# First group of a block-sparse attention and SwiGLU kernel: order of values and transposes, pace of the FFN pieces

## The chip, the core and the metric

The kernel runs on one core of one Trainium2 chip. The metric is device time in microseconds of one execution; the time before is the median of three runs. The engines are TensorE (PE in the profile, its weight loads PEld), VectorE (DVE), ScalarE (ACT), GpSimd (POOL) and SyncE (SP), which issues DMAs, as POOL does too. They run side by side, each in its own order, and wait for each other by semaphores.

## The reference

```python
# q, k, v: (4, 8, 768, 64) float32; block = 32, n_blocks = 24
scores = scale * np.matmul(q, k.transpose(0, 1, 3, 2))
# mask: neighbouring blocks, first and last block row and column,
#       and three sampled key blocks for each query block
scores = np.where(mask, scores, -1000000000.0)
scores = scores - np.max(scores, axis=-1, keepdims=True)
attn = np.exp(scores)
attn = attn / (np.sum(attn, axis=-1, keepdims=True) + 1e-09)
attn_out = np.matmul(attn, v)
x = attn_out.transpose(0, 2, 1, 3).reshape(B * S, H * D)        # 3072 x 512
rms = np.sqrt(np.mean(x * x, axis=-1, keepdims=True) + 1e-06)
xn = x / rms * rms_g
g = xn @ w_gate                                                 # 512 x 1536
out = (g * (1.0 / (1.0 + np.exp(-g))) * (xn @ w_val)) @ w_out   # 1536 x 512
```

## The kernel before

Queries, keys and weights are used in bf16. The work is cut into nine groups: the first batch into three groups of two 128-row chunks of queries, each of the other three batches into two groups of three chunks. The loop goes over the groups (`gi`), and in each over the eight heads (`h`). The order of all instructions is written out by hand: an engine runs what the program says next for it.

For one head, `scores` (L285) multiplies keys by queries in two parts (three in a large group) into one of two score tiles in PSUM. The mask needs no pass of its own: 24 extra rows, in partitions 64 to 87 of the transposed keys `KT` and queries `QT`, add a large negative number to what is masked. ACT takes the exponential of each part into `ex` (L297). `pv` (L301) multiplies `ex` by the values `Vp`, which have a column of ones for the sum, into the tile `op`, and DVE normalizes it into `stage` (L310, L311). In the code before, `pv` of a head comes one head later, behind that head's two parts of scores.

The tile `op` stands in a PSUM pool with a single buffer (`ps_o`, tag `ot`). Another pool (`ps_f`, tag `ff`) has three buffers and holds everything else that TensorE writes: gates, values, down-projections, fillers and some of the transposes.

After the last `pv` of a group, `squares` (L315) and `rms_power` (L323) make the root mean square, `rms_scale` (L334) writes `xs`, and the transposed `xg` comes by TensorE (`transpose_x`, L348) for the three groups of the first batch and for the last group, and by a DMA transpose from SP's queue for the five others. `enter` then puts the group's FFN pieces in a list, `fill`: for each of 12 blocks of 128 hidden columns a gate piece (L375) and a value piece (L386), then for each chunk four down pieces (L403). A head has four places (`position`) from which pieces are drawn:

```python
    def enter(e, positions):
        fill.extend(ffn_pieces(ps_f, e["grp"], e["xg"]))
        rate[0] = len(fill) / positions
```

So the FFN of one group lies between the attention of the next. What is left in the list when attention ends is drained, and the last group's FFN follows.

In the first group there are no pieces yet. Keys and queries of pair 0 (heads 0 and 1) come in float32 by SP's queue and are cast and transposed at once (`first_cast`, `first_turn`, `first_copy`). Pairs 1 to 3 and the values are loaded by POOL's queue in the order k, q, v of each pair, then the weights; from the ninth load on, POOL waits before a load for the landing of the one eight before it. `transpose_qk` (L246) turns a pair of loaded heads by TensorE, `copy` brings the result into `KT` or `QT` (L262). Of the queries, the first chunks are turned ahead of the group that needs them, the rest later (`hi` and `lo`). `cast_v` (L102) casts the values of a pair. `keep_busy` (L145) issues matmuls whose result nobody reads, "fillers" in what follows. `side_work`, `turn_first`, `casts` and `turns` hold what is done beside a head. The other batches are turned by DMA transposes from SP's queue (`turn`, `place`).

Of the kernel before, what the change touches and what calls it, by code (L numbers as in the profile page):

```python
# [18 lines left out]
def kernel(  # L19
# [17 lines left out]
    nc = tc.nc  # L37
    P = 128
    B, H, S, D = q.shape
# [9 lines left out]
    HC = NC // 2  # L49
# [73 lines left out]
    def first_cast(h, which):  # L123
        t16 = ld.tile([P, NC * D], BF16, name="t16", tag="t16", bufs=4)
        nc.scalar.copy(out=t16, in_=first[(h, which)])
        return t16

    def first_turn(t16, lo, hi, unread=None):
# [98 lines left out]
    nc.sync.dma_start(out=QT[0][D:KR, 2:H, 0:2 * P],  # L227
                      in_=qmask[:, 0:2 * P].unsqueeze(1).to_broadcast([NB, H - 2, 2 * P]))
    unread = ps_s.tile([P, 1024], FP32, name="unread0", tag="st")
    keep_busy(8, 256, unread)  # L230
    k16 = first_cast(0, 0)
    kt = first_turn(k16, 0, HC, unread)
    q16 = first_cast(0, 1)
    qt = first_turn(q16, 0, 1, unread)
    keep_busy(5, 256, unread)
    first_copy(0, 0, kt, 0, 0, HC, nc.scalar.copy)
    first_copy(0, 0, kt, 1, 0, HC, nc.vector.tensor_copy)
    first_copy(0, 1, qt, 0, 0, 1, nc.scalar.copy)
    first_copy(0, 1, qt, 1, 0, 1, nc.vector.tensor_copy)
    second16 = [first_cast(1, which) for which in range(2)]  # L240
    mask_keys(HC, NC)
    nc.sync.dma_start(out=KT[0][D:KR, 4:H, :],
                      in_=kind.unsqueeze(1).to_broadcast([NB, H - 4, S]))


    def transpose_qk(pr, which, lo, hi, spare, copy):  # L246

        b = 0  # L250
        src = (kbf if which == 0 else qbf)[(b, pr)]
        dst = (KT if which == 0 else QT)[b % 2]
        pool, tag = (ps_f, "ff") if spare else (ps_o, "ot")
        t = pool.tile([P, 2, HC, P], BF16, name="tqk", tag=tag)
        for e in range(2):
            for cc in range(lo, hi):
                nc.tensor.transpose(  # L257
                    out=t[:, e, cc, :], in_=src[:, e, 2 * cc * D:(2 * cc + 2) * D],
                    identity=ident)
        view = dst[0:D, 2 * pr:2 * pr + 2, :].rearrange("p e (c w s) -> p e c w s", w=2, s=P)  # L260
        for w in range(2):
            copy(out=view[:, :, lo:hi, w, :], in_=t[w * D:(w + 1) * D, :, lo:hi])  # L262
# [180 lines left out]
            if fill:  # L443
                fill.pop(0)()

    prev = None
    ending = None

    def after_pv(e, h):
        if h == H - 2:  # L450
            squares(e, 0, 0, (H - 1) * D)
        if h == H - 1:
            for it in range(e["grp"][2]):
                squares(e, it, (H - 1) * D, H * D)
            rms_power(e)

    def side_work(gi, h):

        if gi == 0:
            if h == 0:  # L460
                copy_rows(KT, kind, 2, 4, 0, S)
            if h % 2 == 0:
                cast_v(0, h // 2, nc.vector)
            if h == 1:
                load_gv(NF // 2, NF)
                nc.gpsimd.dma_start(out=wo, in_=moe_w_out.rearrange("(c p) f -> p c f", p=P))
            if h == 1:
                for third in range(1, FIRST):
                    mask_queries(third)
                nc.sync.dma_start(  # L470
                    out=QT[0][D:KR, 1:H, 2 * P:S],
                    in_=qmask[:, 2 * P:S].unsqueeze(1).to_broadcast([NB, H - 1, S - 2 * P]))
        if gi == 1:
            if h == 1:
                load_qk(1, 0)
                load_v(1, 0)
                load_v(1, 1)
                load_qk(1, 1)
            if h == 3:
                nc.gpsimd.dma_start(  # L480
                    out=gain, in_=moe_rms_g.unsqueeze(0).to_broadcast([P, DM]))
                load_qk(1, 2)
            if h == 5:
                load_qk(1, 3)
        if gi == 2 and h == 1:
            for T, m in ((KT, kind), (QT, qmask)):
                nc.gpsimd.dma_start(out=T[1][D:KR, :, :],
                                    in_=m.unsqueeze(1).to_broadcast([NB, H, S]))

    def turn_first(gi, h):  # L490


        if gi == 0 and h == 0:
            transpose_qk(1, 0, 0, HC, True, nc.vector.tensor_copy)
        if gi == 0 and 0 < h < H - 2:
            if h % 2:
                transpose_qk(h // 2 + 1, 1, 0, 1, True,
                             nc.scalar.copy if h < 4 else nc.vector.tensor_copy)
            else:
                transpose_qk(h // 2 + 1, 0, 0, HC, True, nc.vector.tensor_copy)  # L500
        if gi == 0 and h >= H - 2:
            e = h - (H - 2)
            t = first_turn((q16, second16[1])[e], 1, HC)
            for w in range(2):
                first_copy(e, 1, t, w, 1, HC, nc.vector.tensor_copy)
        if gi == 1 and h in (0, 2, 4):
            transpose_qk(h // 2 + 1, 1, 1, HC, h == 0, nc.vector.tensor_copy)

    def casts(gi, b, g, h):

# [16 lines left out]
    def turns(gi, b, g, h):  # L527


        ready = next(iter(turned), None)  # L530
        if gi == FIRST - 1:
            turn(1, h // 2, h % 2)
        if 0 < b < B - 1 and h >= 4:
            turn(b + 1, 2 * g + (h - 4) // 2, h % 2)
        if ready is not None:
            place(*ready)
# [3 lines left out]
    for gi, grp in enumerate(groups):  # L540
# [8 lines left out]
        for h in range(H):  # L549
            ex = ex_tile(n)  # L550
            thin = gi == 0 or (gi == 1 and h <= TX)
            if gi == 0 and h in (1, 2):
                keep_busy(2, 512)
            scores(grp, h, 0, ex)
            if h == 0 and prev is not None and prev[0]["grp"][2] == HC:
                squares(prev[0], 2, 0, (H - 1) * D)
            if gi == 0 and h == 0:
                scores(grp, h, 1, ex)
                second = [first_turn(t16, 0, 1 if which else HC)
                          for which, t16 in enumerate(second16)]  # L560
                copy_rows(KT, kind, 1, 2, 0, S)
                copy_rows(QT, qmask, 1, 2, 0, 2 * P)
# [34 lines left out]
            if gi == 0 and h == 0:  # L597
                turn_first(gi, h)
# [5 lines left out]
            if gi == 1:  # L604
# [13 lines left out]
            prev = (cur, h, ex)  # L618
    pe, ph, pex = prev
    squares(pe, 2, 0, (H - 1) * D)  # L620
    pv(pe["grp"], ph, pex, pe["stage"])
    after_pv(pe, ph)

    def drain(left):
        while len(fill) > left:
# [44 lines left out]
```

## Time and profile before

| what | value |
|---|---|
| median of three runs | 316.76 us (316.76 to 317.07) |
| profiled execution | 317.04 us |
| its span, first to last instruction | 315.3 us |
| mean granted TensorE clock | 0.997 |
| TensorE busy | 306.1 us (97%) |
| VectorE busy | 202.4 us (64%) |
| ScalarE busy | 207.7 us (66%) |
| fillers (L150) | 43 matmuls, 14.1 us |
| first gate piece starts at | 28.80 us |
| first down piece starts at | 47.9 us |

Times in the trace are microseconds from the start of the span. A row of the timeline gives start, duration, engine, source line, operation, the tile written and those read, the shape, the number of merged instructions, and in brackets how long the engine had been idle and what ended that. Busy times count the rows themselves; matmuls overlap in the array, so the spacing of the starts says more than the length of a row.

### The profile page before, as it was taken

How to read it: one execution, taken by the hardware profiler on the slowest of the kernel's cores; microseconds unless marked ns; L12 is line 12 of the kernel's file. 1: busy time of each engine (PE TensorE's matmuls, PEld its weight loads, DVE VectorE, ACT ScalarE, POOL GpSimd, SP SyncE). 2: the span in 40 equal slices, each digit the busy share in tenths (PEclk: the TensorE clock that was granted, in tenths of full speed). 3: DMA queues.
4: the chain of work that ended last, by engine and by line, in shares of the span. 5: the costliest groups of instructions: out<-in, count | busy, mean ns of one | idle time of the engine just before them, and what ended most of it. 6: DMA issues, size and time to landing. Idle time of an engine off the chain costs nothing.

```text
span 315.3 us, 7295 instructions
## 1 busy us (share of the span) xinstructions
PE 306.1 (97%) x2875; PEld 202.2 (64%) x2875; DVE 202.4 (64%) x560; ACT 207.7 (66%) x337; POOL 50.0 (16%) x75
## 2 busy tenths in 40 slices
PE   7998999999999999999999999999999999989995
PEld 5676886886787566655666566655666566645553
DVE  6778875776478647782767457682767446674850
ACT  6796775877788676657676676666766766723321
POOL 9626032100220122012110122010000100010000
PEclk9999999999999999999999999999999999999998
DMA  6999999995787589615784368615000220002002
GB/s 142 265 246 209 208 268 174 203 174 125 204 151 129 115 185 150 128 23 152 135 158 94 85 166 143 133 30 149 3 2 0 72 81 2 3 6 94 2 0 101
DMA packets 66754, 37.12 MB, mean 118 GB/s; under 512 B 48544, under 2 KB 62312, under 8 KB 66720
## 3 DMA queue, kind: packets, MB, share of 16 engines
q0 software_dynamic: 14976, 17.76, 30.4%
q1 hardware_dynamic: 51708, 18.89, 27.4%
q8 instruction: 22, 0.36, 0.5%
q14 instruction: 12, 0.10, 0.1%
q10 hardware_dynamic: 36, 0.01, 0.0%
HBM read 28.59 MB, written 6.29 MB: 111 GB/s over the span
## 4 chain that ended last, share of the span: by engine, by line
PE 92%; DVE 3%; DMA 2%; ACT 1%; issue 0%; POOL 0%; DVEq 0%; ACTq 0%
PE gp L375 20%; PE vp L386 19%; PE st L294 19%; PE yp L403 19%; PE op L306 11%; PE unread L150 2%; DVE junk L318 2%; DMA first<-in_k_dram 1%; DMA xg<-xs 1%; PE tx L357 1%; PE tqk L257 1%; DVE stage L311 1%; DVE u L390 0%; PE tfirst L131 0%; DVE hps L392 0%
## 5 line engine op out<-in xcount | busy, mean ns | idle before, releaser
L297 ACT ACTIVATE ex<-st 128x768 bf16<-128x768 f32 x192 | 154.2, 812 | 55.6 <-PE st L294 53.6
L294 PE MATMUL st<-QT,KT 88*128 88x384 bf16 (+1 forms) x432 | 94.5, 310 | 0.9 <-DVE QT L262 0.6
L375 PE MATMUL gp<-xg,wg 128*128 128x384 bf16 (+1 forms) x432 | 80.7, 307 | 0.7 <-DMA xg<-xs 0.7
L390 DVE SCALAR_TENSOR_TENSOR u<-th,gp 128x384 bf16<-128x384 bf16 (+1 forms) x108 | 54.8, 508 | 40.3 <-ACT th L379 38.7
L386 PE MATMUL vp<-xg,wv 128*128 128x384 bf16 (+1 forms) x432 | 80.2, 307 | 0.4 <-DVE u L390 0.4
L403 PE MATMUL yp<-wo,hps 128*128 128x512 bf16 (+1 forms) x300 | 74.0, 370 | 0.7 <-DVE hps L392 0.7
L379 ACT ACTIVATE th<-gp 128x384 bf16<-128x384 f32 (+1 forms) x108 | 48.9, 453 | 28.6 <-PE gp L375 28.4
L392 DVE TENSOR_TENSOR hps<-u,vp 128x384 bf16<-128x384 bf16 (+1 forms) x108 | 55.1, 510 | 12.5 <-PE st L294 0.5
L294 PEld LDWEIGHTS <-KT 88*128 88x128 bf16 x432 | 42.0, 99 | 26.1 <-DVE QT L262 0.8
L375 PEld LDWEIGHTS <-wg 128*128 128x128 bf16 x432 | 40.3, 97 | 21.3 <-issue 1.1
L386 PEld LDWEIGHTS <-wv 128*128 128x128 bf16 x432 | 40.5, 97 | 20.8 <-issue 0.8
L306 PEld LDWEIGHTS <-ex 128*128 128x128 bf16 x1152 | 46.1, 98 | 10.2 <-DVE stage L311 0.5
L306 PE MATMUL op<-Vp,ex 128*128 128x65 bf16 x1152 | 48.8, 194 | 0.1
L403 PEld LDWEIGHTS <-hps 128*128 128x128 bf16 x300 | 27.7, 97 | 23.6 <-DVE hps L392 1.2
L310 DVE RECIPROCAL rz<-op 128x3 f32<-128x3 f32 (+1 forms) x72 | 12.5, 174 | 28.8 <-PE op L306 28.4
L326 POOL TENSOR_TENSOR rstd<-ssq,mhalf 128x3 f32<-128x3 f32 (+1 forms) x9 | 7.3, 815 | 146.0 <-DVE ssq L318 146.0
L311 DVE TENSOR_TENSOR stage<-op,rz 128x192 bf16<-128x192 f32 (+1 forms) x72 | 24.1, 335 | 2.5
L409 ACT ACTIVATE yo<-yp 128x512 f32<-128x512 f32 (+1 forms) x25 | 14.4, 576 | 17.0 <-PE yp L403 17.0
L84 POOL DMA_DIRECT2D vraw<-in_v_dram x16 | 11.9, 747 | 70.1 <-DVE Vp L103 54.4
L150 PE MATMUL unread<-idle 128*128 128x512 bf16 (+1 forms) x43 | 14.1, 406 | 1.2 <-DVE idle L143 1.2
L318 DVE CUSTOM_DVE_ANT_0 junk<-stage 128x448 bf16<-128x448 bf16 x24 | 15.0, 623 | 0.6
L338 DVE SCALAR_TENSOR_TENSOR xs<-stage,rstd,gain 128x512 bf16<-128x512 bf16 x15 | 10.4, 747 | 4.4 <-POOL rstd L326 4.4
(59 smaller groups left out, 102.2 us busy)
## 6 DMA issues: line engine op xcount, KB each, us to landing
vraw<-in_v_dram POOLq DMA_DIRECT2D x16, 384.0 KB, 5.8
out_dram<-yo SPq DMA_DIRECT2D x23, 256.0 KB, 2.4
kbf<-in_k_dram POOLq DMA_DIRECT2D x15, 192.0 KB, 6.4
qbf<-in_q_dram POOLq DMA_DIRECT2D x15, 192.0 KB, 6.6
KT<-turned SPq DMA_DIRECT2D x24, 96.0 KB, 3.7
QT<-turned SPq DMA_DIRECT2D x24, 96.0 KB, 2.4
wo<-in_moe_w_out_dram POOLq DMA_DIRECT2D x1, 1536.0 KB, 25.0
wg<-in_moe_w_gate_dram POOLq DMA_DIRECT2D x2, 384.0 KB, 10.6
```

The lines of the kernel that those rows point to most:

```text
L150: nc.tensor.matmul(out=t[:, 0:cols], lhsT=idle[:, 0:P], rhs=idle[:, 0:cols], start=True, stop=True)
L294: nc.tensor.matmul(out=at[:, e, 0:tg], lhsT=KT[b % 2][0:KR, h, jt * P:(jt + 1) * P], rhs=QT[b % 2][0:KR, h, c0 * P:c0 * P + tg], start=Tru ...
L297: nc.scalar.activation(out=ex[:, nj * part:nj * (part + 1), :], in_=at[:, 0:nj, 0:tg], func=AF.Exp, scale=SCALE)
L306: nc.tensor.matmul(out=op[:, it, 0:VW], lhsT=ex[:, jt, it * P:(it + 1) * P], rhs=Vp[b % 2][:, h, jt, :], start=(jt == 0), stop=(jt == NC - 1))
L311: nc.vector.tensor_tensor(out=stage[:, 0:n, h * D:(h + 1) * D], in0=op[:, 0:n, 0:D], in1=rz[:, 0:n].unsqueeze(2).to_broadcast([P, n, D]), ...
L318: nc.vector.tensor_tensor_reduce(out=junk[:, 0:hi - lo], in0=part, in1=part, scale=1.0, scalar=(e["ssq"][:, it:it + 1] if lo else DM * 1e- ...
L375: nc.tensor.matmul(out=gp[:, 0:tg], lhsT=wg[:, c, f * P:(f + 1) * P], rhs=xg[:, c, 0:tg], start=(c == 0), stop=(c == KD - 1))
L379: nc.scalar.activation(out=th[:, 0:tg], in_=gp[:, 0:tg], func=AF.Tanh, scale=0.5)
L386: nc.tensor.matmul(out=vp[:, 0:tg], lhsT=wv[:, c, f * P:(f + 1) * P], rhs=xg[:, c, 0:tg], start=(c == 0), stop=(c == KD - 1))
L390: nc.vector.scalar_tensor_tensor(out=u[:, 0:tg], in0=th[:, 0:tg], scalar=1.0, in1=gp[:, 0:tg], op0=ALU.add, op1=ALU.mult)
L392: nc.vector.tensor_tensor(out=hps[:, f, 0:tg], in0=u[:, 0:tg], in1=vp[:, 0:tg], op=ALU.mult)
L403: nc.tensor.matmul(out=yp, lhsT=hps[:, f, tt * P:(tt + 1) * P], rhs=wo[:, f, lo:hi], start=(f == 0), stop=(f == NF - 1))
```

## The change

In the first group, `pv` comes two heads later instead of one, ahead of the second part of scores; the last head does two. The transposes of pairs 1 to 3 come at other heads and behind the second part of scores, except at head 1. The casts of the values come at heads 1, 3, 5 and 6 instead of 0, 2, 4 and 6. The query copies of pair 2 go from ACT to DVE, as does one cast of pair 0. From head 1 on, the heads of the group have fewer fillers (one each from head 2 on, two at head 1, where there were two, and four at heads 1 and 2); the start has twelve in front instead of eight, and two instead of five ahead of the first scores. The rest of the queries of pairs 1, 2 and 3 is turned at head 7 of group 0 and heads 0 and 2 of group 1, instead of heads 0, 2 and 4 of group 1, and the second of these now takes the single buffer. The first FFN is spread over 44 positions instead of 36, and each later one over 34 instead of 32. Pair 0 of the second batch is turned by TensorE at heads 5 and 6 of the third group, through the single buffer, and no longer by DMA.

```diff
-    keep_busy(8, 256, unread)
+    keep_busy(12, 256, unread)
     k16 = first_cast(0, 0)
     kt = first_turn(k16, 0, HC, unread)
     q16 = first_cast(0, 1)
     qt = first_turn(q16, 0, 1, unread)
-    keep_busy(5, 256, unread)
+    keep_busy(2, 256, unread)
...
-    second16 = [first_cast(1, which) for which in range(2)]
+    second16 = [first_cast(1, 0)]
...
+    copy_rows(KT, kind, 1, 2, 0, S)
+    copy_rows(QT, qmask, 1, 2, 0, 2 * P)
+    second16.append(first_cast(1, 1, nc.vector.tensor_copy))
...
+    def late_pv():
+        e, h, ex = waiting.pop(0)
+        pv(e["grp"], h, ex, e["stage"])
+        after_pv(e, h)
+        return e if h == H - 1 else None
...
         if gi == 0:
-            if h == 0:
-                copy_rows(KT, kind, 2, 4, 0, S)
-            if h % 2 == 0:
+            if h in (1, 3):
                 cast_v(0, h // 2, nc.vector)
+            if h in (5, 6):
+                cast_v(0, h - 3, nc.vector)
...
     def turn_first(gi, h):
-        if gi == 0 and h == 0:
-            transpose_qk(1, 0, 0, HC, True, nc.vector.tensor_copy)
-        if gi == 0 and 0 < h < H - 2:
-            if h % 2:
-                transpose_qk(h // 2 + 1, 1, 0, 1, True,
-                             nc.scalar.copy if h < 4 else nc.vector.tensor_copy)
-            else:
-                transpose_qk(h // 2 + 1, 0, 0, HC, True, nc.vector.tensor_copy)
-        if gi == 0 and h >= H - 2:
-            e = h - (H - 2)
+        dve, act = nc.vector.tensor_copy, nc.scalar.copy
+        if gi == 0 and h in (1, 2, 4):
+            transpose_qk(0, (h + 2) // 2, 0, 0, HC, True, dve)
+        if gi == 0 and h in (1, 3, 5):
+            transpose_qk(0, (h + 1) // 2, 1, 0, 1, True, act if h == 1 else dve)
+        if gi == 0 and h in (5, 6):
+            e = h - 5
             t = first_turn((q16, second16[1])[e], 1, HC)
...
-        if gi == 1 and h in (0, 2, 4):
-            transpose_qk(h // 2 + 1, 1, 1, HC, h == 0, nc.vector.tensor_copy)
+        if (gi, h) in ((0, H - 1), (1, 0), (1, 2)):
+            transpose_qk(0, (1, 2, 3)[gi + h // 2 if gi else 0], 1, 1, HC, gi == 0, dve)
+        if gi == FIRST - 1 and h in (5, 6):
+            transpose_qk(1, 0, h - 5, 0, HC, False, dve)
...
-        if gi == FIRST - 1:
+        if gi == FIRST - 1 and h > 1:
             turn(1, h // 2, h % 2)
...
-            if gi == 0 and h in (1, 2):
-                keep_busy(2, 512)
             scores(grp, h, 0, ex)
...
+                copy_rows(KT, kind, 2, 4, 0, S)
+            if gi == 0 and h >= 2:
+                late_pv()
...
-                    enter(ending, NPOS + 4)
+                    enter(ending, NPOS + 12)
                     ending = None
-            if gi == 0 and h:
+            if gi == 0 and h == 1:
                 turn_first(gi, h)
-            if thin:
+            if gi == 0 and h in (0, 1) or gi == 1 and thin:
                 keep_busy(1, 512)
             position()
             if gi or h:
                 scores(grp, h, 1, ex)
+            if gi == 0 and h > 1:
+                turn_first(gi, h)
             side_work(gi, h)
             position()
...
-            if prev is not None:
-                pe, ph, pex = prev
-                pv(pe["grp"], ph, pex, pe["stage"])
-                after_pv(pe, ph)
-                if ph == H - 1:
-                    ending = pe
+            if gi or h == H - 1:
+                last = late_pv()
+                if last is not None:
+                    ending = last
...
-                enter(ending, NPOS)
+                enter(ending, NPOS + 2)
```

More of the change, by code (lines that the diff above doesn't have):

```diff
@@ L121, with first_cast @@
     gain = const.tile([P, DM], FP32, name="gain")
-    def first_cast(h, which):
+    def first_cast(h, which, copy=nc.scalar.copy):
         t16 = ld.tile([P, NC * D], BF16, name="t16", tag="t16", bufs=4)
-        nc.scalar.copy(out=t16, in_=first[(h, which)])
+        copy(out=t16, in_=first[(h, which)])
         return t16
@@ L243, with transpose_qk @@
                       in_=kind.unsqueeze(1).to_broadcast([NB, H - 4, S]))
-    def transpose_qk(pr, which, lo, hi, spare, copy):
-        b = 0
+    copy_rows(KT, kind, 1, 2, 0, S)
+    copy_rows(QT, qmask, 1, 2, 0, 2 * P)
+    second16.append(first_cast(1, 1, nc.vector.tensor_copy))
+    def transpose_qk(b, pr, which, lo, hi, spare, copy):
         src = (kbf if which == 0 else qbf)[(b, pr)]
@@ L444, in position @@
                 fill.pop(0)()
-    prev = None
+    waiting = []
     ending = None
@@ L466, in side_work @@
                 nc.gpsimd.dma_start(out=wo, in_=moe_w_out.rearrange("(c p) f -> p c f", p=P))
-            if h == 1:
                 for third in range(1, FIRST):
@@ L490, in turn_first @@
     def turn_first(gi, h):
-        if gi == 0 and h == 0:
-            transpose_qk(1, 0, 0, HC, True, nc.vector.tensor_copy)
-        if gi == 0 and 0 < h < H - 2:
-            if h % 2:
-                transpose_qk(h // 2 + 1, 1, 0, 1, True,
-                             nc.scalar.copy if h < 4 else nc.vector.tensor_copy)
-            else:
-                transpose_qk(h // 2 + 1, 0, 0, HC, True, nc.vector.tensor_copy)
-        if gi == 0 and h >= H - 2:
-            e = h - (H - 2)
+        dve, act = nc.vector.tensor_copy, nc.scalar.copy
[5 more added lines that the diff above has]
+            e = h - 5
             t = first_turn((q16, second16[1])[e], 1, HC)
             for w in range(2):
-                first_copy(e, 1, t, w, 1, HC, nc.vector.tensor_copy)
-        if gi == 1 and h in (0, 2, 4):
-            transpose_qk(h // 2 + 1, 1, 1, HC, h == 0, nc.vector.tensor_copy)
+                first_copy(e, 1, t, w, 1, HC, dve)
+        if (gi, h) in ((0, H - 1), (1, 0), (1, 2)):
+            transpose_qk(0, (1, 2, 3)[gi + h // 2 if gi else 0], 1, 1, HC, gi == 0, dve)
+        if gi == FIRST - 1 and h in (5, 6):
+            transpose_qk(1, 0, h - 5, 0, HC, False, dve)
     def casts(gi, b, g, h):
@@ L551 @@
             thin = gi == 0 or (gi == 1 and h <= TX)
-            if gi == 0 and h in (1, 2):
-                keep_busy(2, 512)
             scores(grp, h, 0, ex)
-            if h == 0 and prev is not None and prev[0]["grp"][2] == HC:
-                squares(prev[0], 2, 0, (H - 1) * D)
+            if h == 0 and gi and groups[gi - 1][2] == HC:
+                squares(waiting[0][0], 2, 0, (H - 1) * D)
             if gi == 0 and h == 0:
@@ L560 @@
                           for which, t16 in enumerate(second16)]
-                copy_rows(KT, kind, 1, 2, 0, S)
-                copy_rows(QT, qmask, 1, 2, 0, 2 * P)
                 for which in range(2):
@@ L596 @@
                 scores(grp, h, 2, ex)
-            if gi == 0 and h == 0:
-                turn_first(gi, h)
             position()
@@ L601 @@
                 transpose_x(ending, 1)
-                enter(ending, NPOS)
+                enter(ending, NPOS + 2)
                 ending = None
-            if gi == 1:
+            if gi:
                 turn_first(gi, h)
@@ L617 @@
                                         scalar2=None, op0=ALU.mult)
-            prev = (cur, h, ex)
-    pe, ph, pex = prev
+            waiting.append((cur, h, ex))
+    pe = waiting[0][0]
     squares(pe, 2, 0, (H - 1) * D)
-    pv(pe["grp"], ph, pex, pe["stage"])
-    after_pv(pe, ph)
+    late_pv()
     def drain(left):
```

## The prediction

> **What bounds the kernel now.** I read the page's busy table first, then the chain that ended last, the waits of TensorE, and the timeline of the start and of the places that the diff touches.
>
> ```profile
> PE 306.1 (97%) x2875; PEld 202.2 (64%) x2875; DVE 202.4 (64%) x560; ACT 207.7 (66%) x337; POOL 50.0 (16%) x75
> PE 92%; DVE 3%; DMA 2%; ACT 1%; issue 0%; POOL 0%; DVEq 0%; ACTq 0%
> PE gp L375 <- DMA xg<-xs: 0.7, 1, 0.7
> PE st L294 <- DVE QT L262: 0.6, 1, 0.6
> PE vp L386 <- DVE u L390: 0.4, 1, 0.4
> ```
>
> TensorE is the chain. From the first gate (28.80 us) on, its rows stand end to end, so only three things move the end: when that gate starts, how much TensorE work follows it, and which waits follow it. Group 0 is different: its fillers (43 matmuls, 14.1 us of rows) only fill, and DVE sets the pace there.
>
> ```profile
> 10.76 1.12 DVE L262 COPY KT<-tqk 64x768 bf16<-64x768 bf16 x2
> 16.01 0.17 DVE L310 RECIPROCAL rz<-op 128x2 f32<-128x2 f32 x1 [0.65 <-PE op L306]
> 17.12 1.12 DVE L262 COPY KT<-tqk 64x768 bf16<-64x768 bf16 x2 [0.61 <-PE tqk L257]
> 23.21 0.17 DVE L310 RECIPROCAL rz<-op 128x2 f32<-128x2 f32 x1 [0.54 <-PE op L306]
> 26.09 0.87 DVE L262 COPY QT<-tqk 64x512 bf16<-64x512 bf16 x2
> 27.02 0.77 DVE L344 TENSOR_SCALAR xs<-stage,rstd 128x512 bf16<-128x512 bf16 x2
> 28.80 0.88 PE L375 MATMUL gp<-xg,wg 128*128 128x256 bf16 x4
> ```
>
> From the first key copy of pair 1 (10.76) to the first xs (27.02) are 16.26 us, of which DVE waits 0.65, 0.61, 0.54 and 0.16 (at 19.93): 2.0 in all. So 14.3 us are work, and xs, tx, xg and the gate follow in fixed steps.
>
> **1. The start, to the first gate: -0.2 us (-1.2 to +0.9).** Fillers become 12 + 2 + 2 + 2 of 256 columns instead of 8 + 2 + 2 + 5. Eight take 1.89 us from 1.19, so twelve end near 3.9, where the first transposes (3.90) wait for the cast anyway: no cost. Three fewer ahead of the scores, 0.21 to 0.24 each, let these start at about 5.7 instead of 6.22 (the query copy on DVE ends at 5.52). The exponentials then start at about 6.65 instead of 7.11, the ACT key copy of head 1 behind them ends at 8.6 instead of 9.12, and head 1's scores, no longer behind pair 1's six transposes and three fillers, start at about 8.7 instead of 10.21. Pair 1's transposes follow (keys landed by 8.6, queries at 9.4 by the wait of POOL's tenth load), and its first key copy comes at about 9.6, 1.2 us earlier than 10.76.
>
> But DVE gets more to do between that copy and xs: the value cast of pair 0, which stood ahead of it at 10.16, now follows (0.56); the query copies of pair 2 come over from ACT (2 x 0.28 = 0.56); one more 64x512 query pair is placed before xs (2 x 0.42 = 0.83). That is 14.3 + 1.95 = 16.2, or 25.8 for xs if DVE never waited. It must wait in two new places: pv of head 2 needs the cast of value pair 1, which DVE does just before, and pv of head 4 likewise that of pair 2; pv start to reciprocal is 0.59 (29.73 to 30.32), so 0.6 each. Two key copies still wait for transposes that stand behind scores (now 0.25 each by the rows in between, 0.61 at most). By this xs is at 27.5 at worst, 25.8 at best; I take 26.8, nearer the late end, since both cast waits follow from the order. Scores of head 4 do start earlier (queries of pair 2 land at 13.6, plus transposes and copies: 14.7 instead of 16.26), but this lead shrinks from head to head.
>
> The query turn at the end of group 1's head 0 now takes the single bank that pv uses, where it took one of three before. It waits for DVE's evacuation of the last pv, behind two 0.62 squares: about 1.2 us, with head 1's scores and exponentials queued behind it. Nothing is charged: what stands between it and tx (two scores and a half, two fillers, one pv, 1.8 us) still fits before xs, from the evacuation to which DVE needs 1.5 to 1.8 in any case; uncovered, it costs up to 0.4, which with xs at 27.5 makes the +0.9.
>
> [...] Here the 512-column fillers take 0.63 and 0.58 at 7.93 and 8.62 and 0.38 from 9.78 on, while the granted clock reads 1.00 throughout. [...]
>
> **2. TensorE work after the first gate: +0.4 us.** Pair 0 of batch 1 adds 12 transposes, and four query transposes (pair 2) move ahead of the gate: net 8. Four take from 30.99 to 31.21, 0.055 each: 0.44. Fillers removed all stand before the gate. [...] The rows decide: each lasts 218 ns, but they are spaced by 55. Of the two DMA transposes and four placing DMAs that leave SP's queue, TensorE waited for none (no such wait is listed), so they bring nothing.
>
> **3. The single bank: +1.0 us (0 to +2.4).** After the gate these turns and the tx transposes share it with pv, and each waits for the evacuation before it and holds up the pv after it until DVE has copied. Before, only the turns at heads 2 and 4 of group 1 did; one cost a row.
>
> ```profile
> 38.30 0.44 PEld L306 LDWEIGHTS <-ex 128*128 128x128 bf16 x12 [0.30 <-DVE QT L262]
> 45.59 0.60 PE L386 MATMUL vp<-xg,wv 128*128 128x256 bf16 x4 [0.39 <-DVE u L390]
> 104.94 4.69 SPq L341 DMA_TRANSPOSE xg<-xs  x3
> ```
>
> After, there are the turn at head 2 of group 1 (pieces now come at 0.73 per position instead of 0.89, so one stands between pv and turn where there were two), tx twice at head 2 of group 2, and the new turns at heads 5 and 6, whose key copies are 1.12 instead of 0.87: about four more by 0.25 to 0.3. Zero if pieces cover them, 0.6 each (the reciprocal row's waits) if none do.
>
> **4. Pace of the pieces: +1.2 us (0 to +2.5).** FFN 1 has 32 pieces over 44 positions instead of 36; 36 have passed when the next enters, so 26 are done and 6 left. FFN 2 then runs at 38/34 = 1.12 per position with 6 old ones first, and two stay left over from then on. At the end of the group, 20 positions after entry, DVE has the squares (0.62 each, three in a large group). The 0.39 above is a value piece that waits for u behind such squares. Before, FFN 2 and 3 had 20 of 24 gate and value pieces done there; now 16 and 18. I charge two boundaries at 0.4 to 0.5. In the drain at the end, four instead of two such pieces stand behind squares and evacuations; the wait there (hps, 0.74 at 281.74) grows by an estimated 0.3, half of one u and hps pair (0.55 each). The pieces themselves are the same number; the drained ones cost the same on TensorE.
>
> **5. The xg wait: -0.7 us (-0.7 to 0).** The gate at 111.04 waited 0.72 for the third transpose of xs, issued over the 4.69 us shown. Two left-over pieces (0.65 each) now stand ahead of that gate and cover it.
>
> Weights stay hidden: the last, w_out, is waited for by POOL until 42.60, and its first use (47.9) moves later. Without that cover each us of lateness costs one.
>
> **Sum.** -0.2 + 0.4 + 1.0 + 1.2 - 0.7 = +1.7. The profiled execution took 317.04 (span 315.3, 1.74 around it) and would take 318.7; the median of the runs is 0.28 lower, so I predict 318.5.
>
> **Rivals.**
> A, faster: the lead of the first group survives. For it: head 4's scores come 1.6 earlier, and DVE's 2.0 of idle time could be used up. Against: 1.95 us of DVE work is added to the same stretch. With xs at 25.8 (-1.2), 0.4 of transposes, 0.3 and 0.4 for bank and pace, -0.7: -0.8, or 316.0. It decides where DVE's waits in group 0 fall under about 0.4.
> B, no difference: xs at -0.8, bank 0.5, pace 0.6, the rest as above: 0.0, or 316.8. It is what pieces well spread over positions would give.
> C, much slower: bank and pace at 1.6 each, xs at +0.2, transposes 0.4, xg still 0.4 late (-0.3): +3.5, or 320.3. It needs DVE busy at most of the new places; its 64% mean speaks against, its dense stretch 24 to 28 us for.
>
> **How the numbers follow.** My own case (317.4 to 319.8) has 0.6, A 0.15, B 0.13, C 0.12. Under 0.2% (0.6 us) this kernel's measurement can't tell from no change. So faster 0.15, same 0.13, slower 0.72. The range reaches half of A's cases down, to 316.0, and to 319.8 above, which leaves about 0.07 and 0.12 outside.
>
> **What would show it.** Head 1's scores near 8.7 and head 4's near 14.7, but the first gate near 28.6; waits of tqk and tx for the bank in groups 1 and 2; vp waits for u near 73 and 103; no DMA wait at 111. A first gate at 27.5 or earlier, or none of the waits after it, would make me wrong on the fast side; TensorE waiting for wg, wv or wo, or half-rate fillers after 10 us, on the slow side.

## The result and the profile after

The changed kernel took 320.45 us (median of four executions, 319.97 to 322.62) beside 316.91 us of the kernel before in the same session: ratio 1.0124, 95% interval 1.0077 to 1.0171. The forecast was 318.5 (316.0 to 319.8): the direction was right, the size was not. The profiled execution took 320.30 us with a span of 318.5, so 3.2 us more span than before. (Executions over 1.5% longer than the fastest of their kernel are left out of all comparisons; the profile of experiment 2 and the first one of experiment 5 are of that kind, and these two profiles are not read.)

The page, busy shares and the chain that ended last:

```profile
PE 303.6 (95%) x2860; PEld 200.5 (63%) x2878; DVE 204.7 (64%) x567; ACT 208.8 (66%) x334; POOL 50.2 (16%) x75
PE 81%; DVE 12%; DMA 3%; issue 2%; ACT 1%; DVEq 0%
```

TensorE's share of the chain fell from 92% to 81%, and DVE's rose from 3% to 12%: TensorE now waits at places where it did not. The waits of TensorE (line, what it waited for: us in total, times, longest), start to 30 us:

```profile
PE st L296 <- DMA QT<-QT: 2.1, 1, 2.1
PE st L296 <- DVE QT L264: 1.2, 2, 0.7
...
PE tqk L259 <- DVE stage L313: 1.1, 1, 1.1
PE op L308 <- DVE Vp L103: 0.6, 1, 0.6
```

The third line is the wait for the single bank at the end of group 1's head 0 that step 1 named and charged nothing for. It held nothing up: from the first `xs` (28.09) to the gate it is 1.77 us, before it was 1.78.

From 60 to 110 us, and from there to the end, TensorE waited for the following. Before, only a down piece waited for `hps` and a gate for `xg` there, 0.7 each (both lines are gone):

```profile
PE vp L388 <- DVE u L392: 1.0, 2, 0.6
...
PE vp L388 <- DVE u L392: 1.2, 1, 1.2
```

The largest of all is the wait for `QT<-QT`, and it is in no step of the forecast. The timeline of TensorE shows it, first the kernel before, then the changed one:

```profile
12.36 0.49 PE L294 MATMUL st<-QT,KT 88*128 88x256 bf16 x3
...
16.26 0.49 PE L294 MATMUL st<-QT,KT 88*128 88x256 bf16 x3 [0.28 <-ACT QT L262]
```

```profile
7.98 0.58 PE L296 MATMUL st<-QT,KT 88*128 88x256 bf16 x3
...
11.99 0.49 PE L296 MATMUL st<-QT,KT 88*128 88x256 bf16 x3 [2.06 <-DMA QT<-QT]
...
15.79 0.50 PE L296 MATMUL st<-QT,KT 88*128 88x256 bf16 x3 [0.67 <-DVE QT L264]
...
29.86 0.88 PE L377 MATMUL gp<-xg,wg 128*128 128x256 bf16 x4
```

Head 1's scores do come early (7.98; forecast 8.7, before 10.21). Head 2's scores then stand still for 2.06 us: they need the mask rows of the queries of heads 2 to 7, which one SP transfer (L227, issued at 5.0) brings, and by the trace that landing ends the wait, at 11.99. Before, head 2's scores started at 12.36 and did not wait for it, so it had landed by then, and it left no line in any list of waits. Head 4's scores are at 15.79 (forecast 14.7), and the first gate is at 29.86, 1.06 later than before.

Cutting the span at the first gate gives the two parts of the loss. Before: 315.3 - 28.80 = 286.5 us from the gate on. After: 318.5 - 29.86 = 288.64. So 1.06 is lost ahead of the gate and 2.14 behind it. Where, the busy time of TensorE tells by stretches (stretch: length, busy; then granted clock, DMA share and GB/s); the difference of the first two numbers is idle time:

```profile
29.86:60.00 30.14, 29.31 (x334) 1.00 1.21 191
60.00:110.00 50.00, 48.69 (x531) 1.00 0.79 147
110.00:270.00 160.00, 159.52 (x1443) 1.00 0.45 95
270.00:287.53 17.53, 16.05 (x135) 1.00 0.02 8
```

The same cuts of the kernel before:

```profile
28.80:60.00 31.20, 30.79 (x350) 1.00 1.23 208
60.00:110.00 50.00, 49.99 (x549) 1.00 0.79 157
110.00:270.00 160.00, 159.28 (x1439) 1.00 0.44 94
270.00:283.91 13.91, 13.04 (x117) 1.00 0.03 9
```

By these rows TensorE is idle for 0.83 + 1.31 + 0.48 + 1.48 = 4.1 us between the first gate and the last group's `tx`, and before for 2.0. About 0.7 of the 4.1 is not waiting, however: this trace lacks 16 of the 300 down matmuls (the page counts x284 for L405, and x300 for the same line before), and a missing row leaves a gap of an estimated 0.05, since a down row is 0.38 long and the next starts 0.22 after it (x10 in 2.17 us, 281.74 to 283.91 before). The 0.48 between 110 and 270 us is of that kind (experiment 6).

### The profile page after: what moved, and what is told of

Its sections match the earlier page's. It is cut to its first block, busy times and chain, and to the rows that moved or that the text cites. A ratio compares the mean times of both kernels' runs of the same rounds, so it can differ in the third digit from the quotient of the medians.

```text
span 318.5 us, 7277 instructions
## 1 busy us (share of the span) xinstructions
PE 303.6 (95%) x2860; PEld 200.5 (63%) x2878; DVE 204.7 (64%) x567; ACT 208.8 (66%) x334; POOL 50.2 (16%) x75
## 4 chain that ended last, share of the span: by engine, by line
PE 81%; DVE 12%; DMA 3%; issue 2%; ACT 1%; DVEq 0%
PE yp L405 19%; PE vp L388 17%; PE gp L377 17%; PE st L296 16%; PE op L308 10%; DVE junk L320 3%; DMA QT<-QT 2%; DVE u L392 2%; DVE stage L313 2%; DVE hps L394 2%; DVE KT L264 1%; DVE rz L312 1%; DMA samp_i<-in_sampled_blocks_dram 1%; PE tx L359 1%; PE tqk L259 1%
## 5 line engine op out<-in xcount | busy, mean ns | idle before, releaser
L405 PE MATMUL yp<-wo,hps 128*128 128x512 bf16 (+1 forms) x284 | 71.3, 369 | 0.6
L296 PEld LDWEIGHTS <-KT 88*128 88x128 bf16 x432 | 41.1, 98 | 28.9 <-DVE QT L216 2.4
L405 PEld LDWEIGHTS <-hps 128*128 128x128 bf16 x300 | 28.1, 97 | 23.7
L76 POOL DMA_DIRECT2D kbf<-in_k_dram x15 | 11.1, 738 | 7.7 <-DMA wo<-in_moe_w_out_dram 7.5
L76 POOL DMA_DIRECT2D qbf<-in_q_dram x15 | 11.0, 735 | 1.1 <-PE gp L377 1.1
```

What stands on the lines that cost most here:

```text
L76: nc.gpsimd.dma_start(out=t, in_=src[b, 2 * pr:2 * pr + 2].rearrange("e (p c) d -> p e (c d)", p=P))
L296: nc.tensor.matmul(out=at[:, e, 0:tg], lhsT=KT[b % 2][0:KR, h, jt * P:(jt + 1) * P], rhs=QT[b % 2][0:KR, h, c0 * P:c0 * P + tg], start=Tru ...
L405: nc.tensor.matmul(out=yp, lhsT=hps[:, f, tt * P:(tt + 1) * P], rhs=wo[:, f, lo:hi], start=(f == 0), stop=(f == NF - 1))
```

## The experiments

**Theories.** T1: the loss is a sum of two things: the landing of the mask rows (first group), and the slower pace of the pieces, sized too low in step 4. T2: the waits are only signs; DVE's chain sets the pace of the first group and the pieces are the same work wherever they stand. T3: part of the loss is the TensorE clock, which falls back in the thinner first group (one of the four executions, 322.62, had a mean clock of 0.995, the others 0.999 to 1.0).

**1. The changed kernel again.**

> The changed kernel unchanged, as a control beside the three others. In the two variants that keep its first group's wait of about 2 us for the mask rows (the one with the old paces and the one with the pair turned by DMA), the granted clock read 0.50 for about 3.4 us right behind that wait (14 to 16 us), in the first profile of the changed kernel it read 1.00. Theory 1 (the wait of about 2 us is long enough to let the clock fall back in some executions, by chance): the times fall in two groups some 1.7 us apart, about 320.0 and 322, and the first gate stands at about 29.9 where the clock was kept and near 31.5 where not. Theory 2 (the clock is no part of it): one group, spread under 0.7 us.

Measured: 320.51, 321.49, 321.87 and 322.01 us; ratio 1.0135 (1.0119 to 1.015). Its profile is one of the longer ones (322.01, span 320.2). The timeline of TensorE, and behind it its stretches (length, busy, clock):

```profile
12.44 0.80 PE L296 MATMUL st<-QT,KT 88*128 88x256 bf16 x3 [2.21 <-DMA QT<-QT]
...
31.62 0.88 PE L377 MATMUL gp<-xg,wg 128*128 128x256 bf16 x4
```

```profile
13.00:13.50 0.50, 0.50 (x11) 0.50 1.08 275
...
16.00:16.50 0.50, 0.50 (x16) 1.00 1.00 373
```

The three score matmuls behind the wait take 0.80 instead of 0.49, the granted clock reads 0.50 from about 12.3 to 15.7, and the first gate comes at 31.62 instead of 29.86. Over the eight executions of this kernel, the four with a mean clock of 0.998 or more took 319.97 to 320.6 (mean 320.35), the four with 0.994 or 0.995 took 321.49 to 322.62 (mean 322.0). A clock of 0.50 for 3.4 us of 320 makes a mean of 0.995. So T3 holds: a fall of the clock is worth 1.65 us, and by the mean clock it happened in half of the executions (two of the eight are profiled, one with the fall and one without).

**2. The landing taken away.**

```diff
-    nc.sync.dma_start(out=QT[0][D:KR, 2:H, 0:2 * P], ...)   # mask rows, heads 2 to 7
+    nc.sync.dma_start(out=QT[0][D:KR, 4:H, 0:2 * P], ...)   # heads 4 to 7
+                copy_rows(QT, qmask, 2, 4, 0, 2 * P)        # heads 2 and 3 by DVE
```

> Changed kernel, but the mask rows of the queries of heads 2 and 3 (256 columns) are copied by VectorE ahead of the key rows of the same heads; the SP transfer carries them for heads 4 to 7 only. Theory 1 (a landing that I did not list: the scores of head 2 waited 2.06 us for that SP transfer, and the first group never gets this time back): the wait of 2.06 is gone, head 2's scores start between 10.3 and 10.8 instead of 11.99, the first gate comes at 28.2 to 28.8 instead of 29.86, and the time falls by 1.1 to 1.7 us, to about 319.0. Theory 2 (VectorE sets the pace of the first group, and a wait of TensorE there is only a sign of it): the added copy (about 0.2 us) replaces the wait, the first gate stays within 0.3 of 29.86 and the time within 0.4 us. Theory 3 (the idle 2 us let the clock of TensorE fall back in some runs): the run-to-run spread (319.97 to 322.62 in the first runs) shrinks as well.

Measured: 319.59 to 320.18 us, ratio 1.0077 (1.0056 to 1.0098), and no clock under 0.998: the mean of these five, 319.8, is 1.4 us under that of all eight executions of the changed kernel (321.2). Against the kernel before in the same session they are 2.4 us slower; the four executions of the changed kernel that kept their clock were 3.3 to 3.4 slower in theirs. So with the clock kept 0.9 comes back, as much as at the gate (experiment 5). The gate of this kernel itself is not known. T1 and T3 hold; T2 holds in part, since the wait was 2.06 and only 0.9 of it comes back.

**3. The pace, taken back and put in alone.** First, the changed kernel with the old paces:

```diff
-                    enter(ending, NPOS + 12)
+                    enter(ending, NPOS + 4)
...
-                enter(ending, NPOS + 2)
+                enter(ending, NPOS)
```

> Changed kernel, but with the paces of before: 36 positions for the first FFN, 32 for the others. Theory 1 (my step 4: fewer gate and value pieces are done when the squares come, and more are left for the drain): the waits of vp for u at about 74 and 104 (2.2 us together in the profiled run of the changed kernel) go back to about 0.4, the tail shrinks by 0.3, and the wait of gp for xg (0.7) comes back: 1.0 to 1.8 us faster, about 319.0. Theory 2 (the pieces are the same work wherever they stand, and the waits move to other rows): within 0.4 us of the changed kernel. The first gate must not move (29.86).

Measured: 1.0074 (1.0039 to 1.0108). One execution kept its clock: 318.38; five with 0.993 to 0.995 took 319.13 to 320.09, one with 0.982 took 322.06. In the profile the clock fell, the first gate is at 32.08, and from there to the end it is 318.3 - 32.08 = 286.2 us: 2.4 less than with the new paces, more than the expected 1.0 to 1.8. The wait of `gp` for `xg`, expected back, did not come back. Then the kernel before with nothing but the new paces:

```diff
-                    enter(ending, NPOS + 4)
+                    enter(ending, NPOS + 12)
...
-                enter(ending, NPOS)
+                enter(ending, NPOS + 2)
```

> The kernel before, with only the paces of the change (44 and 34 positions). Theory 1 (the pace alone costs): waits of vp for u of 1 to 2 us appear near 73 and 103, less the xg wait of 0.7: 0.8 to 1.8 us slower than before, 317.7 to 318.7. Theory 2 (the pace only costs together with the reordered first group, which shifts the squares against the pieces): within 0.4 us of before, 316.5 to 317.3, or up to 0.5 faster by the xg wait that goes.

Measured: 331.74 us, ratio 1.0453 (1.0429 to 1.0477), far outside both theories. A wait that neither names, from 30 to 60 us:

```profile
PE tx L357 <- DVE stage L311: 10.3, 1, 10.3
```

The timeline of POOL's queue says why:

```profile
45.34 0.71 POOL L76 DMA_DIRECT2D kbf<-in_k_dram  x1
57.14 0.71 POOL L76 DMA_DIRECT2D qbf<-in_q_dram  x1 [11.08 <-DMA turned<-qbf]
57.87 0.72 POOL L326 TENSOR_TENSOR rstd<-ssq,mhalf 128x2 f32<-128x2 f32 x1
```

A load of queries waits 11.08 us for the DMA transpose of pair 0 of batch 1 (issued at 45.55, landed at 56.6), so by the trace the load had been given the buffer from which that transpose reads; before, the same load started at 45.89 after a wait of 0.57. The power that makes `rstd` stands behind the load in POOL's queue, `xs` waits for it on DVE, and `tx` on TensorE for that. Why the pace changed the choice of the buffer was not traced.

**4. The pair of batch 1.** The changed kernel with that pair turned by DMA again:

```diff
-        if gi == FIRST - 1 and h in (5, 6):
-            transpose_qk(1, 0, h - 5, 0, HC, False, dve)
...
-        if gi == FIRST - 1 and h > 1:
+        if gi == FIRST - 1:
```

> Changed kernel, but pair 0 of batch 1 is turned by DMA again, as in the kernel before. My steps 2 and 3: 12 transposes by 0.055 us (0.66) leave TensorE, and the two turns at heads 5 and 6 of the group, which use the single bank, with about 0.3 of waits each: 0.7 to 1.2 us faster, about 319.5. Rival (these transposes fill places where TensorE waited anyway, or the DMA transposes delay others): within 0.4 us. [...]

Measured: 323.35 us, ratio 1.0179 (1.0151 to 1.0207): slower, not faster. Its profile (span 321.6, clock 0.994) against that of the changed kernel at the same clock (320.2) is 1.4 more, with this wait behind 110 us:

```profile
PE gp L377 <- DMA xg<-xs: 1.9, 1, 1.9
```

The first `xs` is written at 106.88 to 107.6, but SP's queue still has a placing transfer of batch 1 ahead of its transposes (107.15 to 108.42, they start at 108.54); issuing the three then takes 5.22 us instead of 4.19, and they land 3.4 us after their issue (median) instead of 2.5. With the new paces the pair on TensorE is worth its 12 transposes. Then the change without its first group, the kernel before with the new paces and the pair on TensorE (`transpose_qk` is given the batch, as in the changed kernel):

```diff
+        if gi == FIRST - 1 and h in (5, 6):
+            transpose_qk(1, 0, h - 5, 0, HC, False, nc.vector.tensor_copy)
...
-        if gi == FIRST - 1:
+        if gi == FIRST - 1 and h > 1:
...
+                    enter(ending, NPOS + 12)   # was + 4
...
+                enter(ending, NPOS + 2)        # was NPOS
...
-            if gi == 1:
+            if gi:
                 turn_first(gi, h)
```

> The kernel before with the change's other two parts and without its first group: paces 44 and 34, and pair 0 of batch 1 turned by TensorE at heads 5 and 6 of the second group. Theory 1 (the pace and the pair cost what my steps 2 to 5 said, +1.9 together, on their own as well): 318.3 to 319.5 beside 317.0 to 317.5 of before, with waits of vp for u near 73 and 103 of 1 to 2 us, and no POOL load that waits for a transposed pair (the 10.3 us stall of the pace alone is gone). Theory 2 (the whole loss is the first group's): within 0.4 us of before.

Measured: 320.0 us beside 317.3, ratio 1.009 (1.0077 to 1.0103), clock 1.0 in all four executions. The long stall is gone, and two lists of waits (60 to 110 us, and from there on) hold the same lines as the changed kernel:

```profile
PE vp L385 <- DVE u L389: 1.0, 2, 0.6
...
PE vp L385 <- DVE u L389: 1.2, 1, 1.2
```

So pace and pair cost 2.7 us on their own (2.6 from the first gate on), more than the 1.9 of steps 2 to 5. Last, only the first FFN at the new pace:

```diff
-                enter(ending, NPOS + 2)
+                enter(ending, NPOS)
```

> Changed kernel, but only the first FFN over 44 positions; the others over 32 as before. From the traces so far, first gate to end takes 286.2 to 286.5 us with the old paces and 288.6 to 289.1 with 44 and 34. Theory 1 (the first FFN's pace costs it, as the change's words suggest: pieces left over at the boundary drag on): 287.9 or more from the gate, waits of vp for u near 46 and 74 stay. Theory 2 (the pace of 34 of all later FFNs costs it: one more pair of gate and value pieces is left at every boundary and four in the final drain): 286.2 to 286.8 from the gate, the wait at about 104 and the 1.2 at 282 go, and the time is 1.6 to 2.4 below the changed kernel's at the same clock.

Measured: 1.0089 (1.0059 to 1.0119), 318.99 to 319.7 where the clock was kept. In the profile 317.9 - 30.50 = 287.4 us from the first gate on, halfway between 286.2 and 288.6: the 44 and the 34 cost about 1.2 each, so neither theory alone.

**5. The first group alone.** The changed kernel with the edits of experiment 3 (old paces) and 4 (pair by DMA) together:

> Only the reordered first group of the change: paces 36 and 32, pair 0 of batch 1 turned by DMA. Theory 1 (missed landing): the wait of about 2 us of head 2's scores for the mask rows is there, the first gate is 0.8 to 1.1 later than before's 28.80 where the clock is kept, and up to 1.7 more where it falls back; 0.5 to 1.3 slower than before with the clock kept, up to 3 without. Theory 2 (the first group's order is worth what it was meant for, the loss is behind it): equal or faster than before.

Measured: 317.71 and 317.73 us with the clock kept, 319.13 to 320.61 in four executions with 0.987 to 0.995, beside 317.2 for before: ratio 1.0068 (1.0044 to 1.0091). The same with the mask rows of experiment 2:

> The same as the last, and the mask rows of the queries of heads 2 and 3 copied by VectorE (a landing less). Theory 1: the wait of 2 us and the clock's fall go, the first gate comes at 27.8 to 28.5, and the time is 0.3 to 1.2 below before, 1.5 to 3 below the last kernel. Theory 2 (VectorE's chain takes the gain back): first gate 28.8 or later, time equal to before or above.

Measured: 317.14 us, ratio 0.9995 (0.9984 to 1.0007): equal to before; 27.8 to 28.5 at the gate was too early. TensorE's timeline:

```profile
14.86 0.50 PE L296 MATMUL st<-QT,KT 88*128 88x256 bf16 x3 [0.67 <-DVE QT L264]
...
28.93 0.88 PE L377 MATMUL gp<-xg,wg 128*128 128x256 bf16 x4
```

Head 4's scores come at 14.86, nearly the forecast 14.7, and the first gate at 28.93, 0.93 earlier than in the changed kernel but 0.13 later than before. From head 4 to the gate it is 14.07 us (before 28.80 - 16.26 = 12.54), and as long in the changed kernel (29.86 - 15.79). Step 1 had put 28.6 - 14.7 = 13.9 there, for DVE's added work: T2's share. That DVE sets it is argued here, and supported by experiment 7. Small differences between single gates say little: the two kernels of experiments 3 and 4 that have the first group of before reach the gate at 29.13 and 29.24, not at 28.80.

**6. The two repairs together.** The changed kernel with the edits of experiment 2 and the old paces:

> Changed kernel with two edits undone together: mask rows of heads 2 and 3 by VectorE, and the old paces; the pair of batch 1 stays on TensorE. If the two costs add: first gate near 28.9 as in the kernel with the first group alone and these rows, 286.2 from there: span 315.1, time 316.8 to 317.3, equal to before. If they share a cause (less loss by one when the other is gone): 318 or more. The pair on TensorE should take the wait of gp for xg away (0.9 in the kernel with the first group alone).

Measured: 317.29 us, ratio 0.9995 (0.9984 to 1.0006); first gate 29.02, and 315.0 - 29.02 = 285.98 from there. The two costs add. The wait for `xg` is gone here too, at the old paces. The stretches from the gate to the last group's first `tx`, against those shown above:

```profile
29.02:60.00 30.98, 30.59 (x352) 1.00 1.18 220
60.00:110.00 50.00, 49.63 (x548) 1.00 0.77 133
110.00:270.00 160.00, 160.00 (x1441) 1.00 0.46 94
270.00:284.21 14.21, 13.34 (x119) 1.00 0.03 9
```

Idle are 0.39 + 0.37 + 0 + 0.87 = 1.6. For the changed kernel the second profile (experiment 1) is the one to compare with, since its trace has all 300 down matmuls: from its gate to the last group's `tx` (31.62 to 289.24) it has 0.71 + 1.14 + 0 + 1.42 = 3.3 in the same four stretches, and no idle time between 110 and 270 us. From the gate to that `tx` it takes 257.6 us instead of 255.2, so the slower pace costs 2.4 us there, and nothing of it between 110 and 270 us.

The lists of waits name 1.6 of these 2.4. Most of the rest stands at the same places, since a row of a matmul ends after the next could have started (in the changed kernel the scores at 70.38 are x2 in 0.49 and the next row starts at 70.71, 0.16 before their end), and the lists count a wait from that end only. By the starts of the rows in the changed kernel's first profile, `vp` comes late by 0.31 at 66.70 (in no list), 0.54 at 74.93, 0.80 at 105.55 and 1.41 at 282.34. With the old paces `vp` is nowhere behind 60 us more than 0.2 late, and the largest wait there is of a down piece, 0.9 at 282.04.

**7. DVE in the first group.** To that kernel, three edits at once:

```diff
-            transpose_qk(0, (h + 1) // 2, 1, 0, 1, True, act if h == 1 else dve)
+            transpose_qk(0, (h + 1) // 2, 1, 0, 1, True, act if h < 4 else dve)
-        if (gi, h) in ((0, H - 1), (1, 0), (1, 2)):
+        if gi == 1 and h in (0, 2, 4):     # second query turns, as before
...
+            if gi == 0 and h >= 5:         # after side_work, so behind the casts
+                turn_first(gi, h)
```

> The last kernel with VectorE's chain of the first group relieved: the query copies of pair 2 go to ScalarE (0.58 us), the value casts of pairs 2 and 3 stand ahead of the turns of their heads (pv of head 4 waited 0.59 for a cast), and the second query turns stand in the second group again (0.86 of copies off VectorE ahead of xs). Theory 1 (VectorE sets the pace of the first group once the landing is out of the way): first gate at 27.0 to 28.2 instead of 28.9, time 0.7 to 1.9 below the last kernel and 0.5 to 1.7 below before, 315.5 to 316.6. Theory 2 (TensorE's order and ScalarE's exponentials set it): gate within 0.3 of 28.9, no gain.

Measured: 317.25 us, ratio 0.9995 (0.9972 to 1.0019); in the profile (317.91, above the median) the gate is at 29.65, later by 0.63. The cast now stood ahead of the query copies that head 6's scores need, and TensorE's timeline shows what that cost (0.54 before the edit):

```profile
20.48 0.39 PE L296 MATMUL st<-QT,KT 88*128 88x256 bf16 x2 [1.56 <-DVE QT L264]
```

The copies given to ACT cost head 4 1.25 us of waiting for ACT instead of 0.67 for DVE. Less work on DVE, but the wrong piece of it first. So only the order was changed, and only behind what the scores need (`second_turn` holds the lines of the second turns of heads 0 and 1 that stood in `turn_first`, where they ran ahead of the cast):

```diff
             side_work(gi, h)
+            if gi == 0 and h in (5, 6):
+                second_turn(h - 5)
```

> The kernel with the mask rows by VectorE and the old paces (pair of batch 1 on TensorE), and one more edit: at heads 5 and 6 of the first group the value casts of pairs 2 and 3 stand ahead of the second query turns of heads 0 and 1 (first needed in the second group), but behind the copies of pair 3's queries that head 6 waits for. Theory 1 (VectorE's idle time behind a cast that a pv waits for sets the pace: 0.66 at 20.5): the copies of 0.59 fill that idle time, the first gate comes at 28.3 to 28.6 instead of 29.02, 0.4 to 0.7 faster: 316.6 to 316.9 beside 317.3 of both kernels. Theory 2 (the landing of value pair 2, or the squares behind head 6, set it): gate within 0.2 of 29.0 and no gain.

Measured: 316.25 us, ratio 0.9961 (0.9944 to 0.9977): faster than both kernels. DVE's timeline before that edit,

```profile
18.84 0.59 DVE L140 COPY QT<-tfirst 64x256 bf16<-64x256 bf16 x2
19.36 0.55 DVE L103 CAST Vp<-vraw 128x768 bf16<-128x768 f32 x1
20.56 0.17 DVE L312 RECIPROCAL rz<-op 128x2 f32<-128x2 f32 x1 [0.66 <-PE op L308]
```

and with it:

```profile
19.23 0.55 DVE L103 CAST Vp<-vraw 128x768 bf16<-128x768 f32 x1
19.81 0.59 DVE L140 COPY QT<-tfirst 64x256 bf16<-64x256 bf16 x2
20.44 0.17 DVE L312 RECIPROCAL rz<-op 128x2 f32<-128x2 f32 x1
```

The copies fill the 0.66 in which DVE waited for the `pv` that waited for DVE's own cast. In the profiled execution a key landing was 0.61 late (head 4's scores at 15.41 instead of 14.94), so its gate at 28.88 gains only 0.14; from head 4 to the gate it is 13.47 instead of 14.08, 0.61 less. That agrees with the expected 0.4 to 0.7. The medians, 317.29 and 316.25 from two sessions, differ by more (1.0); what the rest of that comes from is not shown.

## Why the forecast was wrong, step by step

The failed steps are 1 and 4, too low by about 1.3 each, and 3, too high by about 1; with them the sum of +1.7 becomes +3.2 where the clock is kept, and +4.9 where it falls (span 320.2). That the forecast was not still lower is due to step 3's error going the other way.

- **Step 1, start to first gate: -0.2 forecast, +1.06 measured, +2.8 with the fallen clock.** The list of landings had keys, queries and values, but not the transfer of the mask rows (L227) that SP issued at 5.0. It lay unseen because head 2's scores started at 12.36 before and did not wait for it (in the five profiles with this wait that are read, it ended between 11.99 and 12.99); the change meant to start them 2 us earlier. The rest of the step held: head 1 at 7.98, nothing lost by the single bank at group 1's head 0, DVE as the pace. With the landing out of the way the gate is at 28.93, 0.3 from the forecast 28.6; the lead of head 4 shrinks on the way, as the step said.
- **The clock.** No step charged a fall of the clock; the forecast has "half-rate fillers after 10 us" only among the signs of being wrong on the slow side. It fell in half of the executions of the changed kernel. Fewer fillers alone did not do it: without the wait, TensorE was busy 4.6 to 4.7 of the 6 us from 6 to 12 (experiments 5 and 6; before 5.89), and of the kernels in which DVE copied the mask rows 2 of 49 compared executions had a mean clock of 0.995 or less. Of those that kept the wait it was 21 of 32. In the changed kernel TensorE was busy 3.32 of these 6 us in the profile that kept its clock, and 3.33 in the one that did not, so the busy time does not tell which. In the three profiles with the fall the clock of 0.50 lasted about 3.4 us, behind waits of 1.81, 2.07 and 2.21 us (experiments 4, 3 and 1); in experiment 1 a 512-column filler took 0.63 at 14.97, within the fall, and 0.38 at 16.70, behind it. What makes the clock fall in one execution and not in the next is open: behind a wait of 2.06 it stayed at 1.00.
- **Step 2, +0.4, and step 3, the single bank, +1.0.** With the old paces and the pair on TensorE, gate to end takes 286.0 to 286.2 us, 0.3 to 0.5 less than before. Of this -0.7 is the gate's wait for `xg`, so steps 2 and 3 together cost 0.2 to 0.4 where +1.4 was charged. The transposes alone were sized at +0.4; the bank cost next to nothing, its waits being two of 0.2 in the lists. Step 2 also had it that the pair's transposes "bring nothing" by leaving SP's queue, and that failed: at the old paces the wait for `xg` is 0.9 with the pair on DMA and the mask rows copied by DVE (second kernel of experiment 5) and absent with it on TensorE (experiment 6); at the new paces the DMA pair costs 1.4.
- **Step 5, -0.7: the right size by the wrong mechanism.** The wait for `xg` is gone, but not because left-over pieces cover it. With these pieces and the pair on DMA it is 1.9 (experiment 4), and without them and the pair on TensorE it is gone (experiment 6).
- **Step 4, the pace: +1.2 forecast, 2.4 to 2.7 measured.** Mechanism and places were right: at 74.9, 105.5 and 282.3 `vp` waits for a `u` that stands behind squares on DVE. The sizes were too low. For the two boundaries 0.9 was charged, and by the starts of the rows they cost 0.54 + 0.80; in the drain +0.3, and it is 1.41 instead of 0.9; the 0.31 at 66.70, where a value piece follows its gate piece at once and no squares stand, was not charged. That is 2.15 of the 2.4 to 2.7; the rest is in smaller delays that were not traced.
- **Rivals.** C (320.3) had the right time by the wrong sum: bank 1.6, pace 1.6, gate +0.2. Its pace was the nearest to the measured 2.4 to 2.7, and its bank cost next to nothing: the time was luck.

## What to carry to other kernels

When a change moves work earlier, list every transfer that the moved work reads, also those that no wait in the old profile names: a landing that comes just in time is invisible until something wants it 2 us earlier (2.06 us of waiting here). A slower pace for interleaved pieces is not free when the pieces form a chain over three engines: the same matmuls, spread thinner, leave TensorE waiting inside the chain where DVE has other work in front of it (2.4 us here, from the first gate to the last group's `tx`). Before idle time is read as waiting, compare the counts of matmuls: a trace can lack some (16 of 300 down matmuls here). And look at what DVE does just before it waits: an operation that others need can go ahead of one that only a later stage needs, which here was worth more than moving work to another engine (ratio 0.9961 beside 0.9995, experiment 7).

## What the runs showed of the hardware

- In three profiles the granted clock read 0.50 for about 3.4 us behind a wait of TensorE of 2.21, 2.07 and 1.81 us (experiments 1, 3 and 4); in the first profile of the changed kernel it read 1.00 behind a wait of 2.06. Of the eight executions of the changed kernel, the four with a mean clock of 0.994 or 0.995 took 322.0 us on average, the four with 0.998 or more 320.35. From 6 to 12 us TensorE was busy 3.32 us in the profile of this kernel without the fall and 3.33 in the one with it.
- In the kernel before with the new paces (experiment 3) a DMA transpose of queries took 11.0 us from issue to landing; from 40 to 60 us the packets of q0 (software_dynamic in the trace) took 79.5% and those of q1 (hardware_dynamic) 36.1% of the 16 DMA engines' span. A load that waited 11.08 us for its source buffer held up POOL's queue, and with it a GpSimd operation of 0.72 us, for which TensorE stood still for 10.3 us.
